# Loading and splitting the first experts' weights in the last attention tiles instead of the first

## The chip, the cores and the metric

One core of a Trainium2 chip runs the whole kernel in one launch. The metric is the device time in microseconds, the median of several runs; lower is better. The engines are TensorE (PE in the rows; PEld is its weight load), VectorE (DVE), ScalarE (ACT), GpSimd (POOL) and SyncE (SP), which issues most transfers.

## The reference

A linear attention with decay feeds a mixture of eight experts with one expert per token, and that feeds a dense layer pair.

```python
# attention: batch 4, heads 8, 768 tokens, head size 48
for t in range(S):
    cur = einsum('bhd,bhe->bhde', u * k[:, :, t], v[:, :, t])
    y[:, :, t] = einsum('bhd,bhde->bhe', r[:, :, t], state + cur)
    state = w[None, :, :, None] * state + einsum('bhd,bhe->bhde', k[:, :, t], v[:, :, t])
# experts: x is [3072, 384], w1 [8, 384, 1024], w2 [8, 1024, 384]
e = argmax(x @ w_gate); p = softmax(x @ w_gate)[e]
x = p * (maximum(x @ w1[e], 0) @ w2[e])
# dense pair: w_in [384, 2048], w_out [2048, 384]
h = x @ w_in
out = (h - tanh(h)) @ w_out
```

## The kernel before, in words

**Attention.** The 768 tokens of each of 4 sequences are cut into 6 chunks of 128; a tile is one chunk of one sequence, so there are 24 tiles (`NN`), `n` = 0 to 23, and one loop goes over them in an order written out by hand (the scheduler is off, each engine runs its instructions as the code issues them). The step of tile n holds work of several tiles: `load(n + 3)` (SP: r, k and v by token, 576 KB, and r and k by dimension, twice 192 KB; five buffers), `diag_sum(n + 1)` and `scale(n + 1)` (VectorE, L338 and L313), `outp(n - 1)` (TensorE: L403 with the state `Sb`, then L408 with the masked scores `am`), `diag(n + 1)` (ScalarE, L345: writes the diagonal of `am`), `state_mm(n)`, `scores(n)` (TensorE, L371 and L354), `mask(n)` (VectorE, L360: puts the scores below the diagonal into `am`), `state_add(n)`, and `side(n + 2)`, `side_kh(n + 2)` (GpSimd: the products `rk`, `rku`, `kh`, L318, L324 and L333). A tile of the first chunk has no state to multiply, one of the last chunk none to make. Once a chunk (every fourth tile) the gate's logits, its choice and the ranks of the tokens follow, in small steps on VectorE. `xout_t` and `xout_g` transpose a finished tile to token order, scale it (ScalarE, L552, tile `xs`) and store it to `xd` in DRAM; seven tiles late at first, later by a table (`XOUT`).

**The head.** After tile 22's step GpSimd gathers the first 256 tokens of expert 0 from `xd` (`head_gather`, L574). After the loop TensorE transposes them (`head_trans`, L585), the last chunk's gate and ranks follow, and `head1(f)` and `head2(f)` begin the first expert's two products on them: `head1(f)` takes the first half and `head2(f)` the second half of the weights of pair f // 2, so `head1(0)` and `head1(1)` need parts 0 and 1 of pair 0.

**The weights.** A pair p holds 256 of the 1024 inner columns of an expert, 128x1536 numbers. `w_load(p, half)` fetches half of it (384 KB) into one of four buffers `stg`, used in turn (SP, L76); the load into a buffer waits until its former content is split. `w_split(p, part, eng)` turns a quarter (128x384) into two parts that together hold the number in TensorE's faster format: ScalarE casts (L84), and VectorE or GpSimd subtracts the cast from the number (L85). Before, the halves of pairs 0 to 2 are loaded in the steps of tiles 1, 3, 5, 7, 9 and 11, pair 0 is split in tiles 3 to 6, three quarters of pair 1 in tiles 21 to 23 and the rest, with half of pair 2, right after tile 23, all with VectorE. Everything on SP stands in one queue, in the order of the code.

After the head come the eight experts and the dense pair, which the diff doesn't touch.

Of the kernel before, what the change touches and what calls it, by code (L numbers as in the profile page):

```python
# [30 lines left out]
def rwkv_moe_moe_kernel(ctx: ExitStack, tc: tile.TileContext, rk_t, rkv, pk, u, wp1, wp2, out):  # L31


    nc = tc.nc
# [31 lines left out]
    def w_load(p, half):  # L66
        t = stgp.tile([P, 768], F32, tag="stg", name="stg")
        if p < PRE:
            src = wp1[p]
        elif p < NP1:  # L70
            r = nc.values_load(wrow[0:1, p:p + 1], engines=(mybir.EngineType.SP,), min_val=0, max_val=NP1 - 1,
                               skip_runtime_bounds_check_because="an expert's pair")
            src = wp1[bass.ds(r, 1)].rearrange("o p x -> (o p) x")
        else:
            src = wdec[p - NP1]
        nc.sync.dma_start(out=t, in_=src[:, half * 768:(half + 1) * 768])  # L76
        stg[p, half] = t

    def w_split(p, part, eng=nc.vector):
        half, n = part // 2, 384  # L80
        sl = slice(part * n, (part + 1) * n)
        of = stg[p, half][:, part % 2 * n:(part % 2 + 1) * n]
        dst = ring[p % RING]
        nc.scalar.copy(out=dst[:, 0, sl], in_=of)  # L84
        eng.tensor_tensor(out=dst[:, 1, sl], in0=of, in1=dst[:, 0, sl].bitcast(F32), op=ALU.subtract)  # L85
        if part % 2:
            stg.pop((p, half))

    def w1_of(i):
        p, c = divmod(i, 2)  # L90
        W = ring[p % RING]
        return lambda s, kk: W[:, s, kk * 256 + c * P:kk * 256 + (c + 1) * P]
# [138 lines left out]
    def load(n):  # L231
        fetch(n, n_b[n % NB], t_b[n % NB])
# [77 lines left out]
    def scale(n):  # L310

        t = t_b[n % NB]
        nc.vector.tensor_tensor(out=t, in0=t, in1=PRK, op=ALU.mult)  # L313
# [22 lines left out]
    def diag_sum(n):  # L336
        dt = at2.tile([P, H], F32, tag="dt", name="dt")
        nc.vector.tensor_reduce(out=dt, in_=st.pop(("rku", n)), axis=AX.X, op=ALU.add)  # L338
        st["dt", n] = dt

    def diag(n):
        dt = st.pop(("dt", n))
        am = at3.tile([P, 2, HP, P], F32, tag="am", name="am")
        for h in range(H):
            nc.scalar.activation(out=am[:, h % 2, h // 2, :], in_=ident, func=ACTF.Copy, scale=dt[:, h:h + 1])  # L345
        st["am", n] = am
# [39 lines left out]
    def state(n):  # L386
        state_mm(n)
        state_add(n)

    def state_copy(n):  # L390
        c, b = seq[n]
        if c == C - 1:
            return
        for q in range(2):
            nc.scalar.copy(out=Sb[b][64 * q:64 * q + 64, :, 64 * q:64 * q + D], in_=Sc[b][64 * q:64 * q + 64, :, :])

    def outp(n):
        c, b = seq[n]
        am = st.pop(("am", n))

        if c > 0:
            for j in range(HP):
                nc.tensor.matmul(Yp[j % 2][:, j // 2, :], lhsT=Sb[b][:, j, :], rhs=t_b[n % NB][:, 0, j, :],  # L403
                                 start=(j < 2), stop=False)
        for j in range(HP):
            for q in range(2):
                p0 = 64 * q
                nc.tensor.matmul(Yp[j % 2][p0:p0 + D, j // 2, :], lhsT=n_b[n % NB][:, 2, 2 * j + q, :],  # L408
                                 rhs=am[:, q, j, :], start=(c == 0 and j < 2), stop=(j >= 2))
        if b == 0:  # L410
            st["y", c] = yp.tile([P, HP, B, P], F32, tag="y", name="y")
        for i in range(2):
            nc.scalar.copy(out=st["y", c].rearrange("p (j i) b t -> p i j b t", i=2)[:, i, :, b, :], in_=Yp[i])
# [106 lines left out]
    def rank_row(c):  # L520
        nc.scalar.activation(out=st["rh", c][:, :, 1, :], in_=st.pop(("hv", c)), func=ACTF.Copy, scale=pid)
# [15 lines left out]
    def xout_t(n, bank=None):  # L537
        c, b = seq[n]
        y = st["y", c]
        if bank is None:  # L540
            ps = ps1.tile([P, HP, P], F32, tag="X", name="Xps", bufs=2)
        else:
            ps = yb[bank].rearrange("p (j t) -> p j t", t=P)
        for j in range(HP):
            nc.tensor.transpose(ps[:, j, :], y[:, j, b, :], ident)
        st["x", n] = ps
# [62 lines left out]
    def head1(f):  # L609
        wf, ps, h2 = w1_of(f), hps[(3, 0, 2, 1)[f % 4]], h2h[f % 3]  # L610
        n = 0
        for a, b in ((0, 0), (1, 0), (0, 1)):
            for kk in range(KD):
                nc.tensor.matmul(ps, lhsT=wf(a, kk), rhs=xth[b][:, kk], start=(n == 0), stop=(n == 8))
                n += 1
        nc.scalar.activation(out=h2[:, 0], in_=ps, func=ACTF.Relu)
        nc.vector.scalar_tensor_tensor(out=h2[:, 1], in0=ps, scalar=0.0, in1=h2[:, 0].bitcast(F32),
                                       op0=ALU.max, op1=ALU.subtract)
# [63 lines left out]
    with tc.manual_schedule():  # L682
# [19 lines left out]
        NN = len(seq)  # L702

        def at_step(n, first, fn):

            m = n - first
            if m >= 0 and m % B == B - 1 and m // B < C:
                fn(m // B)
# [12 lines left out]
        nc.gpsimd.memset(cum[0], 0.0)  # L721
        LAG = 7
        L = C - 1
        LOADS = {1: (0, 0), 3: (0, 1), 5: (1, 0), 7: (1, 1), 9: (2, 0), 11: (2, 1), NN - 1: (3, 0)}
        SPLITS = {**{3 + k: (0, k) for k in range(4)}, **{NN - 3 + k: (1, k) for k in range(3)}}
        LATER = {0: ((3, 0), (3, 1)), 1: ((2, 2), (2, 3)), 2: ((3, 2), (3, 3))}
        XOUT = {NN - 3: (NN - 10, NN - 9), NN - 2: (), NN - 1: (NN - 8, NN - 7), NN: ()}
        for n in range(NN + 1):
            if n == NN:
                w_split(1, 3)  # L730
                w_split(2, 0)
                w_split(2, 1)
            if n + 3 < NN:
                load(n + 3)
            if n in LOADS:
                w_load(*LOADS[n])
            if n + 1 < NN:
                diag_sum(n + 1)
                scale(n + 1)
            at_step(n, 2, logits)  # L740
            at_step(n, 6, rank_q)
            xs_of = [m for m in XOUT.get(n, (n - LAG,)) if m >= 0]
            if xs_of:
                xout_t(xs_of[0])
            if 1 <= n <= NN:
                outp(n - 1)
                at_step(n, 6, rank_row)
                if n > 1:
                    state_copy(n - 1)
            for k, m in enumerate(xs_of):  # L750
                if k:
                    xout_t(m)
                xout_g(m)
            if 0 < n < NN - 1:
                diag(n + 1)
            if n < NN:
                if n > 1:
                    state_mm(n)
                scores(n)
                mask(n)  # L760
                if n == 0:
                    k_table()
                    diag(1)
                elif n == 1:
                    state(0)
                    state(1)
                else:
                    state_add(n)
            if n == 1:
                state_copy(0)  # L770
            if n + 2 < NN:
                side(n + 2)
                if n == 0:
                    side_kh(0)
                    side_kh(1)
                side_kh(n + 2)
            at_step(n, 3, logits2)
            at_step(n, 3, gate)
            at_step(n, 6, idx_mm)
            if n == H0 * B + 3:  # L780
                head_count()
            at_step(n, 4, rank_mm)
            at_step(n, 4, rank_of)
            at_step(n, 5, rank_in)
            if n == H0 * B + 3:
                head_end()
            if n == NN - 2:
                head_gather()
            if n == 0:
                keep_warm(12)  # L790
            if n == 1:
                consts()
                gate_cols()
            if n == 3:
                range_flag(ok)
                nc.vector.tensor_copy(out=e8p, in_=e8)
                nc.vector.tensor_copy(out=thp, in_=thr)
                for t in exs:
                    nc.vector.memset(t[:, :, E:E + 1], 1e-9)
                nc.vector.tensor_reduce(out=sel, in_=ident.rearrange("p (j x) -> p x j", j=HP)[:, 0:E, :],  # L800
                                        axis=AX.X, op=ALU.add)
            if n in SPLITS:
                w_split(*SPLITS[n])

        EARLY = 1
        rank_q(L - 1)
# [28 lines left out]
        logits2(L)  # L835
        gate(L)
        head1(0)
        xout_t(NN - 4, 1)
        xout_t(NN - 3, 2)
        rank_mm(L)  # L840
# [6 lines left out]
        rank_sel(L)  # L847
        rank_q(L)
        rank_row(L)
        head1(1)  # L850
        head1(2)
        idx_mm(L)
# [627 lines left out]
```

## Time and profile before

| what | before |
| --- | --- |
| median of 3 runs (lowest to highest) | 788.3 us (785.2 to 789.77) |
| the profiled execution: its time, its span | 785.56 us, 783.7 us |
| busy, share of the span: TensorE, VectorE, ScalarE, GpSimd | 97%, 82%, 67%, 57% |
| mean granted clock of TensorE, as a share | 0.994 |
| moved by the transfers | 89.84 MB, mean 115 GB/s |

The span is the time from the first to the last instruction. A share of busy time is a mean over stages with different limits: the attention takes about the first 132 us, and what a change there is worth is read from that stretch.

### The profile page before, as it was taken

The page shows a single profiled execution, that of the slowest core. Times are in us where ns is not written, and L with a number is a line of the kernel's source. Part 1 is how long each engine was busy: PE and PEld are TensorE (multiplying, and loading weights), DVE is VectorE, ACT ScalarE, POOL GpSimd, SP SyncE. Part 2 cuts the span into 40 slices and gives each one's busy share as a digit, 9 for nine tenths or more (in the row PEclk, how much of TensorE's full clock was granted, in tenths as well). Part 3 has the DMA queues.
Part 4 walks back from the last instruction along what each step waited for, and adds up shares of the span by engine and source line. Part 5 has one row for each costly group of instructions (what it writes and reads, how often), then busy time and mean ns, then how long its engine had stood idle before and what let it go on. Part 6 is the DMA issues. An engine that isn't in the chain of part 4 may idle for free.

```text
span 783.7 us, 14420 instructions
## 1 busy us (share of the span) xinstructions
PE 763.8 (97%) x5052; PEld 697.1 (89%) x5052; DVE 641.5 (82%) x1125; ACT 525.4 (67%) x1136; POOL 446.1 (57%) x437
## 2 busy tenths in 40 slices
PE   7699999999999999999999999999999999999997
PEld 6678888998899999999889989989998998998887
DVE  6799998778899988984598888888888888888893
ACT  7789998464545544545687776776776777777871
POOL 5989994357768677766264443444435254353533
PEclk9899999999999999999999999999999999999999
DMA  8999983267798999984200000000001000000100
GB/s 199 239 246 284 265 254 120 89 200 207 236 224 266 254 260 275 278 219 132 81 1 2 1 31 11 1 11 31 0 1 41 1 1 21 21 1 0 41 1 40
DMA packets 34975, 89.84 MB, mean 115 GB/s; under 512 B 5690, under 2 KB 13022, under 8 KB 34896
## 3 DMA queue, kind: packets, MB, share of 16 engines
q1 hardware_dynamic: 30704, 78.87, 36.0%
q0 software_dynamic: 4192, 9.99, 4.3%
q8 instruction: 41, 0.67, 0.4%
q14 instruction: 38, 0.31, 0.1%
HBM read 73.10 MB, written 15.74 MB: 113 GB/s over the span
## 4 chain that ended last, share of the span: by engine, by line
PE 50%; issue 2%; ACT 1%; POOL 1%; POOLq 0%
PE h L1314 25%; PE o L1362 23%; PE y L1087 1%; PE hps L1062 1%; POOL out_dram L1375 0%; PE o L1314 0%; POOL g L1351 0%; POOLq L1421 0%; POOL xb L1351 0%; ACT mk L1324 0%; ACT s L1322 0%; POOLq L1475 0%; ACT xb L1350 0%; ACT z L1318 0%; ACT t L1320 0%
## 5 line engine op out<-in xcount | busy, mean ns | idle before, releaser
L1351 POOL TENSOR_TENSOR g<-t,g 128x512 fp32r<-128x512 f32 x93 | 120.4, 1295 | 176.8 <-ACT g L1350 126.6
L1314 PE MATMUL h<-xb,ring 128*128 128x512 f32 x855 | 213.6, 395 | 0.0
L1362 PE MATMUL o<-ring,g 128*128 128x384 f32 x1116 | 209.3, 336 | 0.0
L1362 PEld LDWEIGHTS o<-ring,g 128*128 128x128 f32 x1116 | 196.1, 188 | 8.2
L1314 PEld LDWEIGHTS h<-xb,ring 128*128 128x128 f32 x855 | 159.8, 188 | 30.5
L85 POOL TENSOR_TENSOR ring<-stg,ring 128x384 fp32r<-128x384 f32 x102 | 105.6, 1056 | 55.6 <-ACT ring L84 46.6
L1318 ACT ACTIVATE z<-h 128x512 f32<-128x512 f32 x95 | 56.8, 598 | 96.1 <-PE h L1314 96.1
L1087 PE MATMUL y<-h,ring 128*128 128x256 f32 (+7 forms) x576 | 114.1, 342 | 0.6 <-DVE h L1066 0.6
L1062 PE MATMUL hps<-xt,ring 128*128 128x472 f32 (+6 forms) x504 | 105.6, 353 | 0.1
L1087 PEld LDWEIGHTS y<-h,ring 128*128 128x128 f32 x576 | 101.3, 188 | 4.1 <-DVE h L1066 1.0
L1330 DVE TENSOR_TENSOR t<-t,h 128x512 f32<-128x512 f32 x95 | 65.0, 685 | 40.1 <-ACT t L1320 39.9
L1062 PEld LDWEIGHTS hps<-xt,ring 128*128 128x128 f32 x504 | 90.6, 188 | 3.7 <-DVEq L1201 0.4
L1335 DVE COPY_PREDICATED t<-mk,h 128x512 f32<-128x512 uint32 x95 | 71.4, 752 | 11.0 <-ACT mk L1324 1.3
L84 ACT CAST ring<-stg 128x384 fp32r<-128x384 f32 x152 | 70.4, 513 | 12.2 <-DMA stg<-in_wp_dram 9.5
L1332 DVE SCALAR_TENSOR_TENSOR h<-s,h 128x512 f32<-128x512 f32 x95 | 66.2, 697 | 9.9
L1065 ACT ACTIVATE h<-hps 128x256 fp32r<-128x256 f32 (+7 forms) x64 | 32.0, 500 | 61.8 <-PE hps L1062 59.7
L1322 ACT ACTIVATE s<-z,gb 128x512 f32<-128x512 f32 x96 | 69.6, 725 | 0.0
L1324 ACT ACTIVATE mk<-z,gt 128x512 f32<-128x512 f32 x96 | 69.3, 722 | 0.0
L1333 DVE SCALAR_TENSOR_TENSOR h<-z,h 128x512 f32<-128x512 f32 x95 | 66.1, 696 | 3.3
L1331 DVE TENSOR_TENSOR h<-h,z 128x512 f32<-128x512 f32 x95 | 65.8, 693 | 0.0
L1350 ACT CAST g<-t 128x512 fp32r<-128x512 f32 x93 | 57.6, 620 | 9.0 <-DVE t L1335 6.9
L345 ACT ACTIVATE am<-ident,dt 128x128 f32<-128x128 f32 x192 | 58.6, 390 | 4.9 <-DVE dt L338 4.9
(246 smaller groups left out, 1096.1 us busy)
## 6 DMA issues: line engine op xcount, KB each, us to landing
stg<-in_wp_dram SPq DMA_DIRECT2D x64, 384.0 KB, 4.9
n<-in_rkv_dram SPq DMA_DIRECT2D x24, 576.0 KB, 8.3
d<-in_wp_dram SPq DMA_DIRECT2D x32, 384.0 KB, 5.9
t<-in_rk_t_dram SPq DMA_DIRECT2D x48, 192.0 KB, 8.5
wdec<-dcf SPq DMA_DIRECT2D x32, 192.0 KB, 5.3
xd<-xs SPq DMA_DIRECT2D x24, 192.0 KB, 3.7
stg<-wdec SPq DMA_DIRECT2D x12, 384.0 KB, 4.4
wl<-wdec SPq DMA_DIRECT2D x2, 768.0 KB, 5.1
```

The source lines that it names most:

```text
L84: nc.scalar.copy(out=dst[:, 0, sl], in_=of)
L85: eng.tensor_tensor(out=dst[:, 1, sl], in0=of, in1=dst[:, 0, sl].bitcast(F32), op=ALU.subtract)
L1062: nc.tensor.matmul(ps, lhsT=wf(a, kk), rhs=xt[e][b][:, kk, :], start=(n == 0), stop=(n == 8))
L1087: nc.tensor.matmul(yps[d], lhsT=wf(a)[:, d * P:(d + 1) * P], rhs=h2[:, b, :], start=(f == 0 and n == 0), stop=(f == CH1 - 1 and n == 2))
L1314: nc.tensor.matmul(ps, lhsT=wf(a, kk), rhs=xb[j][:, b, kk, :], start=(n == 0), stop=(n == 8))
L1322: nc.scalar.activation(out=s, in_=z, func=ACTF.Square, scale=G_K ** 0.5, bias=gb)
L1324: nc.scalar.activation(out=mk, in_=z, func=ACTF.Relu, scale=-1.0, bias=gt2)
L1332: nc.vector.scalar_tensor_tensor(out=ps, in0=s, scalar=G_K * G_D, in1=ps, op0=ALU.add, op1=ALU.mult)
L1333: nc.vector.scalar_tensor_tensor(out=ps, in0=z, scalar=G_A, in1=ps, op0=ALU.subtract, op1=ALU.mult)
L1335: nc.vector.copy_predicated(out=t, mask=mk.bitcast(U32), data=ps)
L1351: nc.gpsimd.tensor_tensor(out=g[:, 1, :], in0=ww, in1=g[:, 0, :].bitcast(F32), op=ALU.subtract)
L1362: nc.tensor.matmul(ops[q], lhsT=gg[i][:, b, q * P:(q + 1) * P], rhs=wf(a), start=(f == 0 and n == 0), stop=(f == CH2 - 1 and n == 2))
```

## The change

The table `LOADS` no longer spreads six halves over tiles 1 to 11; it issues four behind the loads of the last tile (in tile 20's step, behind `load(23)`) and one each in the steps of 22, 23 (pair 3's, as before) and behind tile 23. `SPLITS` no longer puts pair 0 into tiles 3 to 6; two quarters each go to tiles 21, 22 and 23, in the order in which the head needs them, and the subtraction is GpSimd's from tile 22 on. Of the three splits that stood behind tile 23 two remain there, one of them on GpSimd; the quarters (1, 2) and (1, 3) move into the head. The number of loads and of splits is the same.

```diff
-        LOADS = {1: (0, 0), 3: (0, 1), 5: (1, 0), 7: (1, 1), 9: (2, 0), 11: (2, 1), NN - 1: (3, 0)}
-        SPLITS = {**{3 + k: (0, k) for k in range(4)}, **{NN - 3 + k: (1, k) for k in range(3)}}
+        LOADS = {NN - 4: ((0, 0), (1, 0), (0, 1), (2, 0)), NN - 2: ((1, 1),), NN - 1: ((3, 0),), NN: ((2, 1),)}
+        SPLITS = {NN - 3: ((0, 0), (0, 1)), NN - 2: ((1, 0), (1, 1)), NN - 1: ((0, 2), (0, 3))}
...
             if n == NN:
-                w_split(1, 3)
-                w_split(2, 0)
+                w_split(2, 0, nc.gpsimd)
                 w_split(2, 1)
...
-            if n in SPLITS:
-                w_split(*SPLITS[n])
+            for k in SPLITS.get(n, ()):
+                w_split(*k, nc.vector if n < NN - 2 else nc.gpsimd)
...
         head1(0)
+        w_split(1, 2)
...
         rank_row(L)
+        w_split(1, 3)
         head1(1)
```

On VectorE, in the steps of tiles 4 and 5, there stood before (`dt` is the sum for the diagonal, `t_126` the r and k of a tile, `A_667` and `A_668` the scores, `Sc_141` the state, `ring_69` pair 0's place):

```order
L383 TENSOR_TENSOR Sc_140<-sw,yh_159 128x192
L85 TENSOR_TENSOR ring_69<-stg,ring_69 128x384
L338 TENSOR_REDUCE dt<-rku 128x8
L313 TENSOR_TENSOR t_126<-t_126,PRK 128x1024
L360 COPY_PREDICATED am<-mlt,A_667 128x512
L360 COPY_PREDICATED am<-mlt,A_668 128x512
L383 TENSOR_TENSOR Sc_141<-sw,yh_159 128x192
L85 TENSOR_TENSOR ring_69<-stg,ring_69 128x384
L338 TENSOR_REDUCE dt<-rku 128x8
```

Now the sum for the diagonal follows the state directly in these steps. In the step of tile 21, where one subtraction for pair 1 (`ring_70`) stood, VectorE has now:

```order
L533 TENSOR_TENSOR idf<-idf,sm 128x32
L535 CAST idxh<-idf 128x2
L85 TENSOR_TENSOR ring_69<-stg,ring_69 128x384 x2
L338 TENSOR_REDUCE dt<-rku 128x8
L313 TENSOR_TENSOR t_128<-t_128,PRK 128x1024
L360 COPY_PREDICATED am<-mlt,A_2050 128x512
```

Two subtractions, of pair 0, precede the sum of tile 23. On SP, from tile 20's load on (`n_133`, `t_128`: tile 23's r, k and v), the queue holds now:

```order
L236 DMA n_133<-in_rkv_dram 128x1152
L238 DMA t_128<-in_rk_t_dram 48x1024 x2
L76 DMA stg<-in_wp_dram 128x768 x4
L554 DMA xd<-xs 128x384 x3
L76 DMA stg<-in_wp_dram 128x768 x2
L554 DMA xd<-xs 128x384 x2
L76 DMA stg<-in_wp_dram 128x768
L814 TENSOR_LOAD flag
L76 DMA stg<-in_wp_dram 128x768
L554 DMA xd<-xs 128x384 x6
```

Before, the three stores of `xs` followed tile 23's load directly, and behind them stood one half, two stores, one half and six stores. On GpSimd, behind tile 23's `kh`, there is now:

```order
L333 TENSOR_TENSOR kh<-n_133,KT 128x384
L574 DMA n_134<-xd,idxh 128x384
L574 DMA n_130<-xd,idxh 128x384
L85 TENSOR_TENSOR ring_70<-stg,ring_70 128x384 x2
L85 TENSOR_TENSOR ring_69<-stg,ring_69 128x384 x2
L85 TENSOR_TENSOR ring_71<-stg,ring_71 128x384
L512 TENSOR_TENSOR hv<-OH,ohh 128x128
```

The five subtractions are new between the gathers for the head (`n_134`, `n_130`) and the rank product `hv`.

## Rows read from the trace of the kernel before

**Rows 1.** Busy time by stretch, granted clock, DMA share, GB/s.
```profile
20.00:40.00 20.00, 14.02 (x202) 11.61 (x199) 14.91 (x27) 14.30 (x47) 19.56 (x40) 0.83 1.03 238
40.00:60.00 20.00, 18.47 (x263) 15.53 (x263) 18.41 (x36) 16.65 (x54) 17.86 (x17) 1.00 1.01 245
...
120.00:140.00 20.00, 19.89 (x238) 17.15 (x235) 15.99 (x55) 16.20 (x46) 6.50 (x8) 1.00 0.45 140
```

**Rows 2.** TensorE in order of time: start, length (us), line, tiles, count.
```profile
43.31 1.16 PE L403 MATMUL yh<-t,Sb 128*128 128x128 f32 x8
...
46.39 1.16 PE L354 MATMUL A<-t 64*128 64x128 f32 x16
...
48.87 1.06 PE L403 MATMUL yh<-t,Sb 128*128 128x128 f32 x8
...
52.11 1.16 PE L354 MATMUL A<-t 64*128 64x128 f32 x16
...
54.04 1.06 PE L403 MATMUL yh<-t,Sb 128*128 128x128 f32 x8
...
57.80 1.16 PE L354 MATMUL A<-t 64*128 64x128 f32 x16
...
60.38 1.06 PE L403 MATMUL yh<-t,Sb 128*128 128x128 f32 x8
...
62.74 1.16 PE L354 MATMUL A<-t 64*128 64x128 f32 x16
...
73.64 1.06 PE L403 MATMUL yh<-t,Sb 128*128 128x128 f32 x8
...
76.58 1.16 PE L354 MATMUL A<-t 64*128 64x128 f32 x16
```

**Rows 3.** VectorE in order of time; in brackets the idle time before, and its releaser.
```profile
41.11 1.00 DVE L85 TENSOR_TENSOR ring<-stg,ring 128x384 fp32r<-128x384 f32 x1 [0.65 <-ACT ring L84]
...
45.89 1.13 DVE L85 TENSOR_TENSOR ring<-stg,ring 128x384 fp32r<-128x384 f32 x1 [0.69 <-ACT ring L84]
...
47.41 2.02 DVE L313 TENSOR_TENSOR t<-t,PRK 128x1024 f32<-128x1024 f32 x1
49.36 1.34 DVE L360 COPY_PREDICATED am<-mlt,A 128x512 f32<-128x512 uint32 x2
```

**Rows 4.** GpSimd in order of time, tiles 6 and 7.
```profile
48.43 1.87 POOL L324 TENSOR_TENSOR rku<-rk,ub 128x384 f32<-128x384 f32 x1
...
53.05 1.00 POOL L318 TENSOR_TENSOR rk<-n 128x384 f32<-128x384 f32 x1 [1.32 <-DMA n<-in_rkv_dram]
```

**Rows 5.** Transfers (36 to 58, 96 to 115 us, whole span): count, KB each, median us to landing.
```profile
n<-in_rkv_dram SPq DMA_DIRECT2D x4, 576.0 KB, 10.4
...
n<-in_rkv_dram SPq DMA_DIRECT2D x4, 576.0 KB, 5.7
...
n<-xd,idxh POOLq DMA_INDIRECT x2, 3.4
```

**Rows 6.** ScalarE and VectorE in order of time, tile 21.
```profile
122.74 0.51 ACT L84 CAST ring<-stg 128x384 fp32r<-128x384 f32 x1
...
123.28 0.56 DVE L85 TENSOR_TENSOR ring<-stg,ring 128x384 fp32r<-128x384 f32 x1 [1.07 <-ACT ring L84]
```

**Rows 7.** SP, GpSimd and TensorE in order of time, the end of the attention.
```profile
111.70 1.99 SPq L238 DMA_DIRECT2D t<-in_rk_t_dram  x2
115.55 5.36 SPq L554 DMA_DIRECT2D xd<-xs  x3
...
125.18 1.08 POOL L574 DMA_INDIRECT n<-xd,idxh  x1 [0.30 <-issue]
...
133.88 0.40 POOL L512 TENSOR_TENSOR hv<-OH,ohh 128x128 f16<-128x128 f16 x1 [7.61 <-DVE ohh L502]
...
162.20 3.41 POOL L85 TENSOR_TENSOR ring<-stg,ring 128x384 fp32r<-128x384 f32 x3 [4.99 <-ACT ring L84]
...
132.11 0.85 PE L585 MATMUL hp<-ident,n 128*128 128x128 f32 x6
```

More of the change, by code (lines that the diff above doesn't have):

```diff
@@ L734, in rwkv_moe_moe_kernel @@
                 load(n + 3)
-            if n in LOADS:
-                w_load(*LOADS[n])
+            for k in LOADS.get(n, ()):
+                w_load(*k)
             if n + 1 < NN:
```

## The prediction

> **What bounds the kernel now.** I read the stretches first (busy time of each engine, DMA share), then TensorE's instructions in order of time through attention tiles 5 to 11, then VectorE's, GpSimd's and the transfers' times to landing over the same tiles, and last the end of the attention. The step of a tile n is what the loop does for n; its `scores` matmuls (L354) mark it on TensorE.
>
> The stretches say that two things are full early on. The DMA engines are busy 1.03 and 1.01 of the time from 20 to 60 us at 238 and 245 GB/s, and only 0.45 from 120 to 140 us [rows 1]. Over 36 to 58 us a tile's 576 KB load takes 10.4 us to land, over 96 to 115 us only 5.7 [rows 5]. TensorE is busy 14.02, then 18.47 of 20 us, and 19.89 at the end [rows 1]: from the middle of the attention on it is nearly dense, so a microsecond saved there or before it stays saved, and one added at the end is paid.
>
> What a microsecond saved is worth I read from the stretch on TensorE from the Sb matmuls (L403) of tile n to the scores of tile n+1. Nothing but the matmuls with the masked scores (L408) and the state matmuls stand between, so it is the same work for each tile with a state; what exceeds the densest one is waiting for VectorE's mask (L360). Dense is 60.38 to 62.74, 2.36 us. In tile 5 it is 43.31 to 46.39, 3.08 us (0.72 too long); in tile 6 48.87 to 52.11, 3.24 (0.88); in tile 7 54.04 to 57.80, 3.76 (1.40). Tile 11, which stands in the gate's chain as tile 7 does but has no weight work beside it, takes 73.64 to 76.58, 2.94 (0.58) [rows 2]. So TensorE loses 3.00 us in tiles 5 to 7.
>
> **The change part by part.**
>
> *What leaves tiles 3 to 6.* Four casts on ScalarE and four subtractions on VectorE (L84, L85). On VectorE a subtraction takes 1.00 us in tile 4 and 1.13 in tile 5, each behind an idle 0.65 and 0.69 us for its cast: 1.65 and 1.82 us in which VectorE's next work stands still. What is late next is the scaling of r and k (L313) in the following step and so the mask behind it: in the step of tile 6 the scaling runs 47.41 to 49.43 and tile 6's mask starts at 49.36 [rows 3], although its scores began at 46.39 and take 1.16 us [rows 2]. Without the two subtractions the mask is about as early as the scores allow, and tile 6's 0.88 us goes. In tile 5 the mask is bound by its own scores, which end as the Sb matmuls begin; its pair takes 1.34 us [rows 3], the Sb matmuls 1.06 [rows 2], so about 0.3 stays and 0.42 goes. In tile 7 the gate's chain keeps the 0.58 that tile 11 shows; 0.82 goes. Sum: 0.42 + 0.88 + 0.82 = **2.1 us**. The bounds are 0 (another engine takes the place) and 3.0 (all the waits go). I take 2.1 because GpSimd, which gives VectorE the sum for the diagonal, is relieved too, next.
>
> *What leaves the transfer queue.* Six halves of 384 KB (0.393 MB) between tiles 1 and 11, of the loads that the queue carries at 245 GB/s, 1.6 us each. Three of them, issued in the steps of tiles 1, 3 and 5, stand ahead of tile 9's load, for which GpSimd waits 1.32 us up to 53.05 [rows 4]; they are 4.8 us, more than the wait, so it goes. Counted alone it gives nothing to TensorE, since it runs beside the chain above; it is why GpSimd doesn't become the limit at once. Where GpSimd's product and VectorE's scaling meet, both grow: 1.87 us from 48.43 [rows 4] beside a scaling of 2.02 [rows 3]. [...]
>
> *The end of the attention.* Ten splits stand there in place of six. Tile 21 gets two on ScalarE and VectorE where it had one. Its VectorE part already waited 1.07 us for the cast that began at 122.74 [rows 6], so the second pair costs one cast more, 0.51 [rows 6], and the diagonal sum and scaling of tile 23 queue behind it; the mask of tile 22, and TensorE behind that, are late by the same. **+0.5 us.** Tiles 22 and 23 have one cast more between them; behind them on ScalarE queue the y copies and the xs copies for the stores. Bounds: 0 if the idle time takes it up, and 1.4 if nearly three casts pass through to TensorE.
>
> The subtractions of tiles 22 to 24 go to GpSimd, five at 1.1 us (3 in 3.41 us later on [rows 7]), 5.7 us in all. They stand behind the second gather for the head, which ends at 126.26, and ahead of the rank product at 133.88 [rows 7]: 7.6 us of idle time hold them. VectorE sheds one in tile 22 and three at the head, which covers what GpSimd may cost it. Parts (1,2) and (1,3) move into the head, a cast and a subtraction each, beside TensorE's dense work; without that cover, 0.5 us each. SP issues four halves behind tile 23's loads, without a wait on a buffer, from 113.69 on; behind them queue three stores of xs, the last of which leaves by 120.91 [rows 7]. Four issues of 0.35 us are hidden there. Loads (1,1), (3,0), (2,1) and (3,1) wait for VectorE or GpSimd; behind them wait only stores whose readers come at the first expert. All cost nothing.
>
> **Sum.** -2.1 + 0.5 = -1.6 us. Against the profiled execution, 785.56 us (span 783.7), that is 784.0. Its time is 2.7 below the median of the runs, 788.3; the mean of these four times is 787.2, and I put the forecast there: **785.6 us**.
>
> **Rivals.**
> *A: no early gain.* VectorE, GpSimd, ScalarE and TensorE are all nearly full, and what leaves one may reappear as a wait for another: GpSimd's line stays, VectorE waits for its sum instead. For it: GpSimd idles hardly more than for the one load. Against it: tiles 8 to 10, with the same work and more, run dense. Time: 787.2 + 0.5 = 787.7.
> *B: more is gained.* All 3.0 us of waits go and the cast in tile 21 hides, and the earlier loads also relieve tiles 8 to 12. 787.2 - 3.0 = 784.2, and with a further 0.6 us 783.6. For it: the queue is full to 60 us and beyond; against it: dense rows from 60.38 on.
> *C: slower, the gather for the head.* The gather reads xs that the three stores write. Four halves are 1.57 MB, 6.4 us at 245 GB/s, so from 113.69 they end at 120.1 if the queue were empty, and about 124 with tile 23's load (0.98 MB, 4.0 us) wholly before them; then the last store lands late by some 3 us. The gathers ended at 126.26 and land 3.4 us later [rows 5], 129.7; the transposes (L585) start at 132.11 [rows 7]. It decides from 2.4 us on; at the whole 6.4 us it would cost 4.0 more: 787.2 - 1.6 + 4.0 = 789.6. Against it: the DMA engines are under half busy there, and the stores leave 5 us and more after the halves. [...]
> *D: held at the end.* GpSimd's five subtractions, 1.1 us each [rows 7], stretch two of VectorE's steps ahead of the last masks and ranks by their whole length, as the product and the scaling stretch each other: 787.2 - 1.6 + 2.2 = 787.8. [...]
>
> **How the numbers follow.** Forecast (gain of 0.8 to 2.6 net) 0.68, A 0.12, B 0.11, C 0.04, D 0.05. Half a per cent, 3.9 us, is about what a measurement of this kernel tells from no change; the runs before spread over 4.6. The forecast, A and D lie within it, B mostly; with the spread of the runs I give faster 0.12, same 0.82, slower 0.06. The range takes the forecast's neighbours and the runs' spread: down to 785.2 - 3.0 = 782.2, rounded in to 782.4, and up to 788.3 with A's 0.5 on top, 788.8.
>
> **What would show it.** Right: the stretch from L403 to the next L354 in tiles 5 and 6 within 0.4 us of 2.36, tile 7 near 2.94; tile 8's scores about 2 us before 57.80; no wait of GpSimd's rk for a load in tiles 5 to 9; DMA share under 0.95 over 40 to 60 us; the transposes of the head about 1.6 us before 132.11. Wrong: the waits stay with GpSimd's sum as releaser (A); the L85 wait in tile 21 grows past 0.5, or L585 waits for a gather (C); TensorE's distance from tile 8's scores to L585 grows by more than 1 us (D).

## Result and the profile after

The changed kernel is slower by about half a per cent: 791.06 us in the median of 20 runs, against 786.75 for the 20 runs of the kernel before that were taken with them; the ratio is 1.0054, with an interval of 1.0038 to 1.0069. A second series (e5 below) gave 1.0034 (1.0018 to 1.0050). With the medians of before, 786.75 and 784.46, that is +4.2 us (3.0 to 5.4) and +2.7 (1.4 to 3.9). The forecast, 785.6, and its range, 782.4 to 788.8, missed it: a gain was expected and a loss came.

The page after: span 788.7 us (783.7 before), mean granted clock 0.989 (0.994), the same bytes moved. Where the 5.0 us of the two profiled executions lie is read from five starts on TensorE: tile 5's Sb matmuls (L403), the scores (L354) of tiles 8 and 22, the head's transposes (L585), and the end.

| stretch on TensorE | before, us | after, us | change |
| --- | --- | --- | --- |
| start to tile 5's Sb matmuls (43.31; 43.35) | 43.31 | 43.35 | +0.04 |
| to tile 8's scores (57.80; 55.41) | 14.49 | 12.06 | -2.43 |
| to tile 22's scores (123.01; 119.72) | 65.21 | 64.31 | -0.90 |
| to the head's transposes (132.11; 133.76) | 9.10 | 14.04 | **+4.94** |
| to the end (783.7; 788.7) | 651.59 | 654.94 | +3.35 |

Of the -0.90, 0.35 lies between the scores of tiles 12 and 22 (46.43 us before, 46.08 after) and is not the change's: e3 below, in which no split moved, takes 46.06 there too.

The early gain is there. TensorE after, in order of time (start, length), in the stretches that answer to [rows 2]:

```profile
43.35 1.16 PE L403 MATMUL yh<-t,Sb 128*128 128x128 f32 x8
...
46.29 1.16 PE L354 MATMUL A<-t 64*128 64x128 f32 x16
48.77 1.06 PE L403 MATMUL yh<-t,Sb 128*128 128x128 f32 x8
...
51.12 1.16 PE L354 MATMUL A<-t 64*128 64x128 f32 x16
53.05 1.06 PE L403 MATMUL yh<-t,Sb 128*128 128x128 f32 x8
...
55.41 1.16 PE L354 MATMUL A<-t 64*128 64x128 f32 x16
```

From L403 to the next L354 it takes 2.94, 2.35 and 2.36 us in tiles 5 to 7; before it was 3.08, 3.24 and 3.76. The stretches (busy time of TensorE, its weight loads, VectorE, ScalarE, GpSimd; granted clock, DMA share, GB/s) show the transfer queue relieved over 40 to 60 us, 0.75 where [rows 1] have 1.01, and three pieces of the end:

```profile
40.00:60.00 20.00, 19.93 (x296) 17.53 (x297) 17.79 (x40) 16.98 (x55) 19.42 (x21) 1.00 0.75 212
...
120.00:124.00 4.00, 2.70 (x29) 2.34 (x28) 1.04 (x3) 3.88 (x13) 0.57 (x1) 0.96 0.14 49
124.00:128.00 4.00, 3.43 (x20) 2.73 (x21) 3.90 (x13) 3.26 (x11) 2.24 (x3) 0.50 0.66 195
128.00:132.00 4.00, 4.00 (x44) 3.17 (x40) 1.50 (x5) 3.48 (x9) 2.82 (x3) 0.68 0.31 33
```

From 120 to 124 us TensorE, VectorE and GpSimd all stand still for part of the time, and from 124 to 128 us TensorE runs at half its clock (granted 0.50). What they wait for begins on SP and ScalarE. First SP's queue after, then ScalarE, in order of time (in brackets the idle time before, and its releaser):

```profile
110.43 1.84 SPq L76 DMA_DIRECT2D stg<-in_wp_dram  x4
112.37 8.18 SPq L554 DMA_DIRECT2D xd<-xs  x3
```

```profile
116.20 0.58 ACT L552 ACTIVATE xs<-Xps,gt 128x384 f32<-128x384 f32 x1
119.62 0.58 ACT L552 ACTIVATE xs<-Xps,gt 128x384 f32<-128x384 f32 x1 [2.84 <-PE yh L408]
120.10 2.43 ACT L345 ACTIVATE am<-ident,dt 128x128 f32<-128x128 f32 x8
122.44 0.91 ACT L84 CAST ring<-stg 128x384 fp32r<-128x384 f32 x2
123.25 0.63 ACT L413 COPY y<-yh 128x256 f32<-128x256 f32 x2
```

The two xs of tile 21's step are those of tiles 14 and 15. Before, ScalarE wrote them back to back:

```profile
119.47 1.05 ACT L552 ACTIVATE xs<-Xps,gt 128x384 f32<-128x384 f32 x2
```

Now the second comes 2.84 us late. `xs` has two buffers (pool `gp`), so xs(15) takes the buffer of xs(13), whose store was issued at 112.37, right behind four halves. The releaser that the row names, L408, cannot be it: in the code those matmuls follow xs(15), which reads only the transposes of tile 15 (L545, below), and these had ended at 116.13. What else xs(15) waits for is the store of xs(13). Its landing is not on record in this trace, but in e5, the same kernel, it is: issued at 111.20 and landed 7.4 us later, at 118.6, where xs(15) starts at 118.66. Behind xs(15) on ScalarE stand tile 22's diagonal (L345), the two casts (L84) and the copies that free the `yh` banks (L413), and so VectorE and TensorE wait in turn. VectorE, then TensorE:

```profile
122.96 1.05 DVE L85 TENSOR_TENSOR ring<-stg,ring 128x384 fp32r<-128x384 f32 x2 [4.03 <-ACT ring L84]
...
125.53 1.32 DVE L360 COPY_PREDICATED am<-mlt,A 128x512 f32<-128x512 uint32 x2
```

```profile
115.47 0.66 PE L545 MATMUL Xps<-ident,y 128*128 128x128 f32 x4
...
119.72 1.16 PE L354 MATMUL A<-t 64*128 64x128 f32 x16
...
123.66 2.07 PE L403 MATMUL yh<-t,Sb 128*128 128x128 f32 x8 [1.30 <-ACT y L413]
126.30 2.55 PE L408 MATMUL yh<-am,n 128*48 128x128 f32 x16 [0.57 <-DVE am L360]
...
133.76 0.87 PE L585 MATMUL hp<-ident,n 128*128 128x128 f32 x6
```

TensorE idles 1.30 and 0.57 us, and the matmuls behind that take about twice as long as at the full clock (L403 1.06 and L408 1.08, in e9 below): 2.07 and 2.55 us.

The last stretch's +3.35 lies at the hand-over from the head to the first expert. ScalarE, then TensorE:

```profile
156.44 0.37 ACT L606 CAST ring<-fx 128x256 fp32r<-128x256 f32 x1 [0.86 <-PE fx L605]
159.94 0.37 ACT L606 CAST ring<-fx 128x256 fp32r<-128x256 f32 x1 [3.14 <-PE yh L624]
```

```profile
157.31 0.38 PE L605 MATMUL fx<-ident,n 128*128 128x128 f32 x2
...
160.83 4.98 PE L1063 MATMUL hps<-ring,ring 128*128 128x256 f32 x27 [2.07 <-DVE ring L607]
```

The third cast starts 2.63 us after the transposes that it reads; the second one started 0.42 after its own (156.02). TensorE before, and the stretch from 160 to 164 us after:

```profile
157.30 3.49 PE L1062 MATMUL hps<-ring,ring 128*128 128x256 f32 x27 [0.22 <-DVE ring L607]
```

```profile
160.00:164.00 4.00, 3.17 (x16) 3.17 (x17) 0.85 (x2) 1.62 (x5) 0.00 (x0) 0.66 0.82 249
```

TensorE idles 1.85 us longer (2.07 for 0.22), and the same 27 matmuls then take 1.49 us longer (4.98 for 3.49) at a granted clock of 0.66: together 3.34, all but 0.01 of this stretch's loss.

### The profile page after: what moved, and what is told of

Its sections match the earlier page's. It is cut to its first block, busy times and chain, and to the rows that moved or that the text cites. A ratio compares the mean times of both kernels' runs of the same rounds, so it can differ in the third digit from the quotient of the medians.

```text
span 788.7 us, 14423 instructions
## 1 busy us (share of the span) xinstructions
PE 767.6 (97%) x5052; PEld 700.9 (89%) x5052; DVE 637.5 (81%) x1120; ACT 525.7 (67%) x1136; POOL 452.0 (57%) x442
## 4 chain that ended last, share of the span: by engine, by line
PE 50%; issue 2%; ACT 1%; POOL 1%; POOLq 0%
PE h L1315 24%; PE o L1363 23%; PE y L1088 1%; PE hps L1063 1%; POOL out_dram L1376 0%; PE o L1315 0%; POOL g L1352 0%; POOLq L1422 0%; POOL xb L1352 0%; ACT s L1323 0%; ACT mk L1325 0%; POOLq L1476 0%; ACT xb L1351 0%; ACT z L1319 0%; ACT t L1321 0%
## 5 line engine op out<-in xcount | busy, mean ns | idle before, releaser
L85 POOL TENSOR_TENSOR ring<-stg,ring 128x384 fp32r<-128x384 f32 x107 | 110.5, 1055 | 61.4 <-ACT ring L84 52.6
L84 ACT CAST ring<-stg 128x384 fp32r<-128x384 f32 x152 | 69.9, 512 | 12.0 <-DMA stg<-in_wp_dram 9.2
L345 ACT ACTIVATE am<-ident,dt 128x128 f32<-128x128 f32 x192 | 58.6, 389 | 3.9 <-DVE dt L338 3.9
```

## Experiments

**Theory T1:** the store of xs(13) is held in SP's queue behind the halves, ScalarE waits for its buffer, and everything behind ScalarE is late. **T2:** the casts and subtractions that were added to tiles 21 to 23 fill the engines. **C** of the prediction: the store counts through the gather that reads it. All runs, measured by TensorE from tile 22's scores to L585, which leaves out what executions differ by earlier on; "landing" is the time from the issue of the store of xs(13) to its landing, where the trace has it (-: not on record):

| run | halves ahead of the store of xs(13) | landing, us | ScalarE's wait at xs(15) | tile 22's scores to L585 | ratio to before (interval) |
| --- | --- | --- | --- | --- | --- |
| before | none | 2.9 | none | 123.01 to 132.11: 9.10 | 1 |
| after | four | - | 2.84 | 119.72 to 133.76: 14.04 | 1.0054 (1.0038 to 1.0069) |
| e1_store_first | none | 3.3 | none | 120.42 to 130.34: 9.92 | 0.9982 (0.9963 to 1.0001) |
| e2_third_xs | four, three buffers | 7.4 | none | 118.98 to 128.71: 9.73 | 0.9979 (0.9962 to 0.9996) |
| e3_extra_loads | four extra, on before | 6.6 | 3.07 | 120.42 to 134.59: 14.17 | 1.0054 (1.0033 to 1.0074) |
| e4_early_loads | none | 2.6 | none | 120.23 to 129.63: 9.40 | 0.9984 (0.9967 to 1.0002) |
| e5_changed_again | four | 7.4 | 2.96 | 118.65 to 133.24: 14.59 | 1.0034 (1.0018 to 1.0050) |
| e6_three_ahead | three | - | 1.77 | 118.40 to 130.18: 11.78 | 1.0022 (1.0007 to 1.0038) |
| e7_fill_pe | four | 6.9 | 2.47 | 119.19 to 139.82: 20.63 | 1.0122 (1.0097 to 1.0148) |
| e8_spread | none (one before tile 19's store) | 3.6 | none | 120.30 to 129.26: 8.96 | 1.0004 (0.9989 to 1.0020) |
| e9_fill_free | four | - | 3.08 | 119.84 to 132.75: 12.91 | 1.0021 (1.0010 to 1.0033) |
| e10_two_ahead | two | 5.2 | 0.80 | 119.39 to 130.01: 10.62 | 0.9995 (0.9983 to 1.0006) |
| e11_one_a_tile | one, of the tile before | 5.5 | 1.11 | 119.41 to 129.60: 10.19 | 0.9983 (0.9973 to 0.9993) |

With no half right ahead the store lands after 2.6 to 3.6 us, with two after 5.2, with four after 6.6 to 7.4. The times in the expectations of e1 to e4 were reckoned from 791.1 and 786.75; in the series in which these four ran, the kernel before takes 784.05.

**e1_store_first: the halves behind the store.**

```diff
-            for k in LOADS.get(n, ()):
-                w_load(*k)
+            if n != NN - 4:
+                for k in LOADS.get(n, ()):
+                    w_load(*k)
...
                 xout_g(m)
+            if n == NN - 4:
+                for k in LOADS[n]:
+                    w_load(*k)
```

> The changed kernel, with the four weight halves of tile 20's step issued behind that step's xs store instead of ahead of it. Theory T1 (the store of xs(13) queues behind four halves, so its buffer comes free late, ScalarE waits 2.84 us to write xs(15), and the diagonal, the casts and TensorE's last tiles behind it are late): the wait before ScalarE's second xs of tile 21 falls under 0.5 us, the head's transposes (L585) start near 129 us in place of 133.76, and the time falls by 3 to 5 us from the changed kernel's 791.1, to about 786 to 788. Rival T2 (the casts and subtractions that were added to tiles 21 to 23 hold the engines by themselves): the wait goes, but L585 stays within 1 us of 133.76 and the time within 1 us of 791.1. The loss of about 3.4 us at the hand-over to the first expert (ScalarE's third Relu, L606, at 159.94) has no explanation yet; if it is tied to the store it goes too, and the time is 783 to 785.

SP's queue and ScalarE in that kernel:

```profile
112.98 0.34 SPq L554 DMA_DIRECT2D xd<-xs  x1
113.38 2.14 SPq L76 DMA_DIRECT2D stg<-in_wp_dram  x4
```

```profile
116.90 1.05 ACT L552 ACTIVATE xs<-Xps,gt 128x384 f32<-128x384 f32 x2
```

The same bytes go through the same queue right behind that store (113.38 against 112.98) and not ahead of it, the two xs are back to back, and the time is 782.86 against 784.05 of before. L585 started at 130.34, a little over the 129 that was expected. T2 falls as the cause of the loss: every cast and subtraction of the change is still there.

**e2_third_xs: the halves stay ahead, `xs` has a third buffer.**

```diff
-        xs = pool.tile([P, H, D], F32, tag=tag, name="xs")
+        xs = pool.tile([P, H, D], F32, tag=tag, name="xs", **(dict(bufs=3) if tag == "xs" else {}))
```

> The changed kernel, with three buffers for xs where it has two; the loads stay where the change put them. T1: ScalarE no longer waits before the second xs of tile 21, L585 starts near 129 to 131 us and the time is 786 to 788, although the stores still land late. If instead the lateness of the stores counts through the gather that reads them (rival C of the prediction), L585 or the gather's wait stays as in the changed kernel (133.76; 3.63 us on GpSimd) and the time is 790 to 791. T2 (added casts and subtractions): within 1 us of 791.1.

ScalarE again, and the time from issue to landing of the three stores that it lets go in tiles 20 and 21:

```profile
115.44 1.05 ACT L552 ACTIVATE xs<-Xps,gt 128x384 f32<-128x384 f32 x2
```

```profile
DMA to landing us min/median/max: 3.3/3.3/7.4
```

One store, that of xs(13), still takes 7.4 us to land where the median is 3.3, and ScalarE no longer waits for it: 782.56 us, 1.5 under before. So what costs is the wait for the buffer, and not the lateness of the data; C's gather accounts for at most the 0.26 us for which L585 is idle here (0.44 in e1).

**e3_extra_loads: the cost alone, on the kernel before.**

```diff
+            if n == NN - 4:
+                for k in range(4):
+                    extra = dram.tile([P, 768], F32, name=f"extra{k}")
+                    nc.sync.dma_start(out=extra, in_=wp1[k // 2][:, k % 2 * 768:(k % 2 + 1) * 768])
```

> The kernel before, with four extra loads of 384 KB each (into DRAM scratch that nobody reads) in tile 20's step, where the change puts its four halves; no split is moved. T1: ScalarE waits 2 to 3 us before the second xs of tile 21 here too, L585 starts 3 to 5 us behind 132.11, and the time is 789 to 791.5 against 786.75. T2: ScalarE's wait may appear but the time stays within 1 us of the kernel before.

```profile
120.55 0.58 ACT L552 ACTIVATE xs<-Xps,gt 128x384 f32<-128x384 f32 x1 [3.07 <-PE yh L408]
```

788.54 us against 784.05: with no split moved, four transfers ahead of that store cost 4.2 us by the ratio. T1 holds from both sides. (The row names L408 again, as in after.)

**e4_early_loads: the splits moved, the loads not.** The first four halves are loaded in tiles 1, 3, 5 and 7, as before.

```diff
-        LOADS = {NN - 4: ((0, 0), (1, 0), (0, 1), (2, 0)), NN - 2: ((1, 1),), NN - 1: ((3, 0),), NN: ((2, 1),)}
+        LOADS = {1: ((0, 0),), 3: ((0, 1),), 5: ((1, 0),), 7: ((1, 1),), NN - 2: ((2, 0),), NN: ((2, 1), (3, 0))}
...
-        w_load(3, 1)
...
         w_split(1, 3)
+        w_load(3, 1)
```

> The changed kernel's splits with loads (0,0), (0,1), (1,0), (1,1) at their old places in tiles 1 to 7, so that no halves stand ahead of the stores of tile 20. T1: no wait before the second xs of tile 21. If the early gain (2.4 us by tile 8) came from the casts and subtractions that left tiles 3 to 6, it stays whole: tile 8's scores start near 55.4 us, and the time is 784 to 787. If it came from the transfer queue, tile 8's scores start near 57.8 and the time is 786.5 to 788.5. T2 (the added casts and subtractions cost the end): 789 or more.

TensorE, tile 5's Sb matmuls and tile 8's scores:

```profile
42.72 1.16 PE L403 MATMUL yh<-t,Sb 128*128 128x128 f32 x8
...
54.78 1.16 PE L354 MATMUL A<-t 64*128 64x128 f32 x16
```

12.06 us, as in after; the kernel before and e3 take 14.49. The early gain comes wholly from the splits, and none of it from the transfer queue, which with four of the six halves at their old places moves 258 GB/s over 40 to 60 us (DMA share 0.93). (The starts themselves differ between executions by 2 us and more before tile 5, so only distances are compared.) The time, 782.82, is also that of e1 and e2.

**e5_changed_again: the hand-over.** The kernel is unaltered.

> The changed kernel again, unaltered, for its hand-over to the first expert: ScalarE's third cast for that expert (L606) stood idle for 3.14 us in the profile of after, and from the head's transposes (L585) to the end that profile takes 654.9 us where the kernel before and the four runs so far take 651.6 to 651.8. If the stall belongs to the program, L606 waits about 3 us again, the distance is near 655 and the ratio to before is near 1.0054 again. If it was chance in one execution, L606's last idle is under 1 us, the distance is near 651.6 and the ratio is 1.002 to 1.003 (+2.43 of the wait's tail less the early gain, about +1.6 us).

```profile
118.66 0.58 ACT L552 ACTIVATE xs<-Xps,gt 128x384 f32<-128x384 f32 x1 [2.96 <-DMA xd<-xs]
...
157.21 0.37 ACT L606 CAST ring<-fx 128x256 fp32r<-128x256 f32 x1 [0.92 <-PE fx L605]
```

The hand-over stall is gone (784.8 - 133.24 = 651.56 us to the end), as in all other profiles here (651.5 to 652.0). So the program doesn't bring it in every execution; its cause stays open, and so does how many of the first series' unprofiled runs had it. Their mean granted clock is 0.988 (that of after's profile 0.989), that of e5's runs 0.992, so it may be part of why the first series shows the larger loss. The wait at xs(15) came again, and here the row names the store itself. The ratio, 1.0034, is a little over the 1.002 to 1.003 that was expected for this case.

**e6_three_ahead and e10_two_ahead: the dose.** Of the four halves, the last one or the last two are issued behind the store.

```diff
-            for k in LOADS.get(n, ()):
+            for k in LOADS.get(n, ())[:3]:
                 w_load(*k)
...
                 xout_g(m)
+            for k in LOADS.get(n, ())[3:]:
+                w_load(*k)
```

> The changed kernel with three of tile 20's four halves ahead of the xs store and the fourth behind it. T1: each half ahead of the store costs its landing about 1.6 us, so ScalarE's wait before the second xs of tile 21 shrinks from 2.84 to about 1.2 us, L585 lies between 130.3 (store first) and 133.8 (four ahead) once the start is subtracted, and the time is 784 to 787. If the wait comes from something other than the halves ahead of the store, it stays at 2.8 us.

> The changed kernel with two of tile 20's halves ahead of the xs store and two behind it. T1: from four to three halves ahead ScalarE's wait shrank from 2.84 (2.96) to 1.77 us, 1.1 to 1.2 a half; so two leave about 0.6 us, TensorE hardly idles, its clock stays, and from tile 22's scores to L585 it takes 9.9 to 10.8 us (store first 9.92, three ahead 11.78, four ahead 14.04 and 14.59). The time is 782.5 to 785.5.

ScalarE in e6, then in e10:

```profile
117.22 0.58 ACT L552 ACTIVATE xs<-Xps,gt 128x384 f32<-128x384 f32 x1 [1.77 <-DMA xd<-xs]
```

```profile
117.24 0.58 ACT L552 ACTIVATE xs<-Xps,gt 128x384 f32<-128x384 f32 x1 [0.80 <-PE sm L528]
```

Two, three, four halves: 0.80, 1.77 and 2.84 (2.96) us of wait, about 1.0 to 1.2 for each. (In e10 too the row names a matmul that xs(15) doesn't read; the store, issued at 111.92, landed 5.2 us later, at 117.1.) The landings say the same: 3.3, 5.2 and 7.4 us with none, two and four ahead (e1, e10, e5). That is less than the 1.6 us by which the prediction priced a half. The transfers after, in 40 slices of 0.2 us from 112 to 120 us, fit that:

```profile
GB/s 279 307 230 200 256 225 138 195 184 251 205 230 302 338 307 384 369 384 384 369 384 446 369 415 430 399 384 384 384 399 376 315 254 131 92 77 46 15 0 82
```

Most slices from 115 to 118 us show 370 to 430 GB/s, not the 245 of the early tiles, and 0.393 MB at 390 GB/s is 1.0 us.

**e7_fill_pe and e9_fill_free: the wait and the clock apart.** Unread matmuls stand where TensorE idles, ahead of tile 22's Sb matmuls and of its masked ones; in e9 the same edit writes `yb[2][:, 384:512]`. (In both, L403 are the unread matmuls, two records for each, so x18 and x20; the Sb matmuls are L408 and the masked ones L414.)

```diff
+        def fill(k):
+            for _ in range(k if n == len(seq) - 2 else 0):
+                nc.tensor.matmul(sm[:, 384:512], lhsT=ident, rhs=ident, start=True, stop=True)
+
+        fill(9)
         if c > 0:
...
+        fill(10)
         for j in range(HP):
```

> The changed kernel with 19 matmuls that nobody reads, put where TensorE idles in tile 22's step: 9 ahead of its Sb matmuls and 10 ahead of its masked ones. ScalarE's wait for the store stays. If the fall of TensorE's granted clock (0.50 over 124 to 128 us) adds to the loss what the idle time itself does not, the clock stays near 1.00 there, the masked matmuls take about 1.34 us instead of 2.55, and L585 comes 1.5 to 2 us earlier against tile 8's scores (78.35 us apart in after). If the waits alone make the loss, the distance stays at 78.3 within 0.3.

```profile
127.39 4.16 PE L403 MATMUL sm<-ident 128*128 128x128 f32 x18 [5.56 <-DVE cum L466]
```

That one failed as a test: the bank `sm` holds the gate's small tiles, and the first unread matmul waited 5.56 us for VectorE's work on them. It put a new wait in the place of the old. e9:

> The same 19 unread matmuls in tile 22's step as in the run before, now written to a bank that no other instruction of these tiles uses, so that they wait for nothing. ScalarE's wait for the store stays near 2.9 us. If the fall of TensorE's clock adds to the loss, the granted clock stays near 1.00 over 124 to 128 us, the masked matmuls of tile 22 take about 1.34 us in place of 2.55, and from tile 22's scores to L585 it takes 12 to 13 us in place of the 14.04 and 14.59 of the changed kernel's two profiles. If the waits alone make the loss, it stays at 14.0 to 14.6.

```profile
122.31 2.17 PE L403 MATMUL yh<-ident 128*128 128x128 f32 x18
124.32 1.06 PE L408 MATMUL yh<-t,Sb 128*128 128x128 f32 x8
125.22 2.40 PE L403 MATMUL yh<-ident 128*128 128x128 f32 x20
127.54 1.08 PE L414 MATMUL yh<-am,n 128*48 128x128 f32 x16
```

```profile
124.00:128.00 4.00, 4.00 (x41) 3.88 (x41) 3.90 (x11) 3.16 (x11) 2.45 (x2) 1.00 0.57 173
```

ScalarE waits as long as ever (3.08), the granted clock stays at 1.00, the Sb matmuls take 1.06 us in place of 2.07 and the masked ones 1.08 in place of 2.55. The stretch is 12.91, so in these profiles the clock was some 1.1 to 1.7 of the 4.9 to 5.5 us, and more if the fill had cost nothing. The unread matmuls themselves took back some of it: VectorE's masks begin here at

```profile
125.85 1.34 DVE L360 COPY_PREDICATED am<-mlt,A 128x512 f32<-128x512 uint32 x2
```

and in after the masked matmuls began 0.77 us behind that, here 1.69.

**e8_spread: the early splits put into tiles 12, 13, 16 and 17,** on the kernel before.

```diff
-        LOADS = {1: (0, 0), 3: (0, 1), 5: (1, 0), 7: (1, 1), 9: (2, 0), 11: (2, 1), NN - 1: (3, 0)}
-        SPLITS = {**{3 + k: (0, k) for k in range(4)}, **{NN - 3 + k: (1, k) for k in range(3)}}
+        LOADS = {9: (0, 0), 10: (0, 1), 11: (1, 0), 12: (1, 1), 15: (2, 0), 19: (2, 1), NN - 1: (3, 0)}
+        SPLITS = {12: (0, 0), 13: (0, 1), 16: (0, 2), 17: (0, 3), **{NN - 3 + k: (1, k) for k in range(3)}}
```

> The kernel before with one thing changed: the four splits of tiles 3 to 6 stand in tiles 12, 13, 16 and 17, with the loads in tiles 9 to 19, one to a tile; the end of the attention is as before. If the early gain comes from the splits leaving tiles 3 to 6, the distance from tile 5's Sb matmuls to tile 8's scores is 12.06 us in place of 14.49. If the later tiles then hold the splits beside their other work, the distance from tile 8's scores to L585 stays at 74.3 and the time is 781.5 to 783 against 784 to 787 of before; if they are as full as the early ones, the gain is given back there.

VectorE at the split of tile 17's step, then TensorE at tile 18's masked matmuls:

```profile
100.89 0.93 DVE L85 TENSOR_TENSOR ring<-stg,ring 128x384 fp32r<-128x384 f32 x1 [1.26 <-ACT ring L84]
```

```profile
104.92 0.42 PE L408 MATMUL yh<-am,n 128*48 128x128 f32 x2 [0.68 <-DVE am L360]
```

The early gain is whole (41.78 to 53.84, 12.06 us), and the end is as before (8.96), but tile 8's scores to tile 22's take 66.46 us where before has 65.21: 1.25 of 2.43 us is given back in the later tiles, where VectorE waits 1.26 for a cast as it did early on [rows 3]. What is left of the gain at L585 (87.48 us from tile 5's Sb matmuls, 88.80 before) does not show in the time, 784.49 against 784.46, whose interval is -0.9 to +1.6 us.

**e11_one_a_tile: a version against both.** One half a tile in tiles 18 to 23, behind that tile's store; one split in tiles 20 and 21 each, two in 22 and 23.

```diff
+        LOADS = {NN - 6: ((0, 0),), NN - 5: ((0, 1),), NN - 4: ((1, 0),), NN - 3: ((2, 0),), NN - 2: ((1, 1),),
+                 NN - 1: ((3, 0),), NN: ((2, 1),)}
+        SPLITS = {NN - 4: ((0, 0),), NN - 3: ((0, 1),), NN - 2: ((0, 2), (1, 0)), NN - 1: ((0, 3), (1, 1))}
```

> A version meant to beat both: one half a tile in tiles 18 to 23, each behind that tile's xs store, and the splits one a tile from tile 20 (two in tiles 22 and 23, on GpSimd as in the change). By T1 no store waits behind a half for long, ScalarE does not wait for its second xs of tile 21, and from tile 22's scores to L585 it takes 9.0 to 9.6 us, as before; the early gain stays whole or is in part held by GpSimd's line after tile 9 (0 to 1.4 us). Time 1.3 to 2.7 us under the kernel before.

```profile
117.60 0.58 ACT L552 ACTIVATE xs<-Xps,gt 128x384 f32<-128x384 f32 x1 [1.11 <-DMA xd<-xs]
```

782.76 us against 784.32 of before: faster, by 0.5 to 2.1 us (the interval times that median). The wait was expected to be gone and is not, and with one half it is longer than with e10's two: so the count of halves right ahead of the store is not all. The half of tile 19's step stands ahead of tile 23's load, which lands 7.8 to 8.0 us after issue here (its r and k by dimension 6.0 to 6.3 in e10), and the store stands behind both. TensorE's granted clock stays at 1.00 and the stretch is 10.19 where 9.0 to 9.6 was expected.

## Why the prediction was wrong, point by point

**The step that failed** is the one on the four halves: "behind them queue three stores of xs, the last of which leaves by 120.91. Four issues of 0.35 us are hidden there", and "All cost nothing". It priced the issues and the time at which the last store leaves SP, and not when the first of them lands and who waits for that. The first waits in the queue behind 1.57 MB (7.4 us to landing in e5, 3.3 in e1 with none ahead); ScalarE needs its buffer two xs later. The stretch grew by 4.9 and 5.5 us in the two profiles (14.04 and 14.59 against 9.10), of which 0.5 belong to the splits, and 4.5 and 5.0 to the wait.

**Rival C** had the right mechanism with the wrong waiter. It counted the store through the gather of the head, found 2.4 us of slack there, and gave it 0.04. ScalarE had less slack: in e1 the store landed at 116.3 and ScalarE came to xs(15) at 117.4, so 1.1 us were to spare, and two halves ahead already made it wait (0.80 us). e2 tells the two apart. That C's price, 2.4 us over its base of 787.2, comes near the 2.7 measured in e5 is luck: it was reckoned for another path. That a store is held behind the halves in its queue no row of before shows; the runs show it, with 3.3 us to landing with none ahead (e1), 5.2 with two (e10) and 7.4 with four (e5), about 1.0 us for each half.

**The early gain, -2.1,** was right in mechanism and off in size: 2.43 by tile 8 (12.05 to 12.21 us there in every execution without the early splits, 14.49 in the two with them). Tile 6 gave 0.89 (0.88 forecast), tile 5 only 0.14 (0.42), and tile 7 all of its 1.40 (0.82): the 0.58 that the gate's chain was to keep there did not stay. That the queue's relief counts for nothing here was right (e4). Part of the gain is given back behind tile 8 in some executions, which is rival A's mechanism. From tile 4's scores to tile 12's before takes 38.91 us and e3, with the early splits, 38.65; after, e4, e6, e8 and e9 take 36.16 to 36.65, but e1, e2, e5, e7, e10 and e11 37.51 to 37.60. In e1 VectorE, freed of its own work, waits for GpSimd's product:

```profile
63.78 0.55 DVE L338 TENSOR_REDUCE dt<-rku 128x8 f32<-128x384 f32 x1 [1.40 <-POOL rku L324]
```

So 1.3 to 2.75 us is what the early move is worth against before (1.0 to 2.5 against e3). Why one execution shows this wait and the next doesn't was not settled.

**The second cast and subtraction in tile 21, +0.5,** were right: from tile 22's scores to tile 23's before takes 5.32 us, and e1, e2 and e4, which have all moved splits and no wait at xs(15), take 5.79 to 5.80. TensorE before, then in e4:

```profile
128.33 1.16 PE L354 MATMUL A<-t 64*128 64x128 f32 x16
```

```profile
126.02 1.16 PE L354 MATMUL A<-t 64*128 64x128 f32 x16
```

**Rival D** had its mechanism and not its price. The product and the scaling that it went by take 1.00 (the median of L324) and 1.21 us (the shortest L313) elsewhere in before, so where they met each grew by 0.8 to 0.9. While GpSimd subtracts, a small step of VectorE's ranks (L462) takes 0.60 us after (0.61 to 0.66 in e1, e2 and e4) for 0.16 before: 0.44 to 0.50 more, and no run shows on it the 1.1 us that D put on each of two steps. VectorE before, VectorE after, GpSimd after:

```profile
128.14 0.16 DVE L462 TENSOR_TENSOR cums<-cum,bump 128x8 f16<-128x8 f16 x1
```

```profile
128.31 0.60 DVE L462 TENSOR_TENSOR cums<-cum,bump 128x8 f16<-128x8 f16 x1
```

```profile
127.90 1.95 POOL L85 TENSOR_TENSOR ring<-stg,ring 128x384 fp32r<-128x384 f32 x2 [1.46 <-ACT ring L84]
```

VectorE then waits for TensorE's scores in any case (0.72 us in e1, 0.75 before), and from tile 23's scores to L585, without L585's own idle time, e1, e2 and e4 take 3.61 to 3.68 us for 3.78 before.

**The signs.** What came: tile 8's scores 2.39 us earlier, DMA share 0.75 over 40 to 60 us, tile 6 within 0.4 us of 2.36, and no wait of GpSimd's rk for a load in tiles 5 to 9. What didn't: tile 5 (2.94), tile 7 (2.36, and not near 2.94), and the transposes of the head, later and not earlier. Of the signs of being wrong, tile 21's L85 wait grew to 4.03 us, and the distance from tile 8's scores to L585 by 4.04 (78.35 for 74.31), which was to mean D. Without the store's wait the first is 0.19 to 1.07 us and the second grows by 1.53, 1.38 and 0.54 (e1, e2, e4): what is given back behind tile 8 in e1 and e2, and the 0.5.

The sum with the measured terms: -1.3 to -2.75, +0.5, and the store's wait at 4.5 to 5.0, together +2.2 to +4.2 us; measured were +2.7 and +4.2. The match is of two ranges only: after's profile has -2.4 and +4.9, and the stall of 3.35 beside them, e5's -1.4 and +5.5, so the terms of neither profile add up to the number of its own series. Without the wait the forecast's -1.6 lies in every interval: e1, e2 and e4 measured -1.4, -1.6 and -1.3 us by the ratios, and only e2's interval (-3.0 to -0.3) is clear of no gain at all.

## What to carry to other kernels

When transfers are moved, look in the queue at what stands behind them, and ask for each store not only who reads its data but who needs its buffer back: with two buffers that is an instruction two turns on, on an engine with its own line behind it. The cure is cheap, an issue order with the store first or a third buffer, and either took away the whole loss of 2.7 to 4.2 us; the gain of some 1.5 that was left is, of these two, clear of noise for the third buffer alone. What a wait at TensorE costs is more than its length if the clock falls behind it, as in after (granted 0.50 behind waits of 1.30 and 0.57 us, and the Sb matmuls at 2.07 us for 1.06 in e9), so read the granted clock over the next few microseconds too.

## What the runs showed of the hardware

- TensorE idled 1.30 and 0.57 us in after, 1.42 and 1.33 in e5, and ran at a granted 0.50 over the 4 us from 124; with 19 unread matmuls in the gaps (e9) it stayed at 1.00. In e6, with 0.23 and 1.41 us idle, it stayed at 1.00 as well.
- The transfers moved 370 to 430 GB/s in most slices from 115 to 118 us, behind tile 23's load, against 245 over 40 to 60 us before; here a price per transfer that was read from one stretch did not hold in another (1.6 us for a half, 1.0 to 1.2 measured).
- Of the thirteen profiled executions one, that of after, held ScalarE's third cast at the hand-over until 2.6 us behind the start of the transposes that it reads; the twelve others show 651.5 to 652.0 us from L585 to the end.
- A VectorE step of 0.16 us (L462) took 0.60 to 0.66 us beside GpSimd's subtractions.
- Matmuls in the format of the split weights, 256 columns each, took 129 ns apiece before (L1062, 27 in 3.49 us); those on f32, 128 columns each and two records for each, took 265 ns (L403, four in 1.06 us).
